# Two of four row-block transposes moved from the DMA crossbar to TensorE, and the tail loads re-slotted, in a fused attention and MLP kernel

## The chip, the cores and the metric

One NeuronCore of a Trainium2 chip runs the whole program. The metric is device microseconds of one execution. TensorE (PE in the profile), VectorE (DVE), ScalarE (ACT), GpSimd (POOL) and SyncE (SP) each work through a queue of their own in program order. Here SP only issues DMAs.

## What is computed

`q`, `k` and `v` have the shape 8 x 8 x 576 x 64 (batch, heads, sequence, head dimension), in float32. The reference does attention in a causal window of 64 positions, puts the heads side by side, and then does a residual MLP on rows of 512:

```python
mask = (rel >= 0) & (rel < 64)                      # rel = query position - key position
attn = softmax(where(mask, q @ k.T / sqrt(64), -1e9))
x = concat_heads(attn @ v)                           # 8 x 576 x 512
xn = (x - mean) / sqrt(var + 1e-6) * g_ln
out = x + relu(xn @ w_ch1) @ w_ch2                   # w_ch1 512 x 2048, w_ch2 2048 x 512
```

## The kernel before

**Groups and periods.** The rows are cut into nine groups. Groups 0 to 7 are the first 512 positions of one batch each; group 8 collects the last 64 positions of all eight batches, the "tails". A tail i (0 to 3) holds batches 2i and 2i+1 and makes one block of 128 rows of group 8. A group has four row blocks of 128. The kernel runs the groups' MLPs one after another; I call the time of one group's MLP a period. While period g runs, TensorE also does the attention of the next group b = g+1, in small pieces between the MLP's pieces.

**The MLP of a period** (`mlp_units`, from g = 2) is 30 units: 16 units of the first layer (`l1`, line 437, four 128x512 matmuls each, emptied with ReLU by ACT at line 441 into `hrT`), then 14 units of the second layer (`product`, line 513, eight 128x256 matmuls each, seven products in two halves, combined from PSUM by DVE at line 528 into `osb`). The products take sums `sw` that DVE makes (`presum`, line 427). The product tile `wX` stays in one of the two PSUM buffers of the pool `ps_t` from unit 16 to unit 29.

**Slots.** The order of everything else is written by hand: `at(i, f, ...)` puts a step behind unit i. The same order holds on all engines, because each engine runs its own instructions in the order of the program. For a row block j of the next group the steps are `s_mm` (scores, line 292), `s_exp` (ACT), `s_mask` (DVE, line 319), `b_step` (probabilities times v, line 335, then normalisation and statistics on DVE, lines 338 to 345), `r_step` (1/sqrt of the variance on ACT, lines 354 and 355), `z_step` (the normalised rows z in fp16, DVE, line 365), and a transpose of z into `zT`, which the next period's first layer reads. In `steps` the b_steps of the four blocks stand at slots 4, 8, 12 and 17, and the z_steps at 6, 10, 14 and 20.

**Two ways to transpose z.** `x_step` (line 390) has SP issue one DMA transpose of 128x512 through the crossbar. `zt_step` (line 373) has TensorE do four 128x128 transposes (line 379) into a PSUM tile `ztp` of the pool `ps_t`, and ACT copy it into `zT` (line 382). Before the change, the groups 3 to 7 and the tails use `x_step` for all four blocks; groups 0 to 2 use `zt_step`.

**The queue of SP in a period** g (2 to 5) is: loads of q and k of batch g+2 (`load_qk`, lines 83 and 90, slots 1 and 2), loads of v (`load_v`, line 152, slot 5), x_step of block 0 (slot 7), of block 1 (11), of block 2 (15), the crossbar transposes of q and k of batch g+2 (`x_main(n, 0)`, lines 245 and 251, one DMA for q and two for k, slot 18), x_step of block 3 (20), and `x_main(n, 1)` (21). A step that waits holds all that stand behind it. The casts to fp16 that `x_main` waits for are on ACT (`cast_q`, line 129, slots 16, 16, 17, 19), as are those of v (`cast_v`, slots 21 to 24), on which two copies on POOL's queue (`make_vB`, lines 180 and 181, slot 25) wait. The stores (line 398) are on POOL's queue too, two per period.

**Tails.** The dictionary `TAILS` holds the steps of the tails in periods 6 and 7: loads (`load_tail`, part 0 for q and k: lines 101 and 103, part 1 for v: line 108), casts (`cast_tail`, three per tail, for tails 0 and 3 on POOL, for tails 1 and 2 on ACT), crossbar transposes (`x_tail`, lines 261 and 262), scores and the rest. The tails' tiles share buffers with the batches' tiles: two for q, two for k, one for v.

Of the kernel before, what the change touches and what calls it, by code (L numbers as in the profile page):

```python
# [18 lines left out]
def kernel(  # L19
# [649 lines left out]
    def tail_casts(i, act, *us):  # L669
        return tuple((u, cast_tail, i, part, act) for part, u in enumerate(us))  # L670

    TAILS = {
        6: ((0, load_tail, 0, 0), (0, load_tail, 0, 1), (6, load_tail, 1, 0), *tail_casts(0, False, 8, 9, 10),
            (10, x_tail, 0), (10, load_tail, 1, 1), *tail_casts(1, True, 16, 17, 18), (18, x_tail, 1),
            (15, s_mm, 8, 0), (16, s_mask, 8, 0), (26, b_step, 8, 0),
            (15, load_tail, 2, 0), (21, load_tail, 2, 1), (23, load_tail, 3, 0),
            *tail_casts(2, True, 24, 25, 26), (25, x_tail, 2),
            (27, s_mm, 8, 1), (28, s_mask, 8, 1)),
        7: ((0, x_step, 8, 0), (1, load_tail, 3, 1), (2, b_step, 8, 1), (2, s_mm, 8, 2), (4, s_mask, 8, 2),
            (5, x_step, 8, 1), (7, b_step, 8, 2), (10, x_step, 8, 2), *tail_casts(3, False, 5, 6, 8), (8, x_tail, 3),  # L680
            (12, s_mm, 8, 3), (14, s_mask, 8, 3), (17, b_step, 8, 3), (20, x_step, 8, 3)),
    }
    for g in range(NGRP):
        units = mlp_units(g, (8, 16)[g] if g < 2 else 0, g == 0)
# [2 lines left out]
        def at(i, f, *a):  # L687
            slots[min(i, len(slots) - 1)].append((f, a))
# [6 lines left out]
        def score(u, sg, sj):  # L695
            late = u < 15
            at(u, s_mm, sg, sj, False, None, late)
            if late:
                at(u + 1, s_exp, sg, sj)
            at(u + 1 + late, s_mask, sg, sj)  # L700

        def steps(bg, bj, ub, us, sg, sj):
            if us is not None:
                score(us, bg, bj)
            late = ub < 15
            at(ub, b_step, bg, bj)
            if sj < 4:
                score(ub, sg, sj)
            at(ub + 2, r_step, bg, bj)
            at(ub + 2 + (not late), z_step, bg, bj)  # L710
            at(ub + 3, x_step, bg, bj)

        b = g + 1
        if g == 0:
# [72 lines left out]
        if g > 1 and b < B:  # L787
            for j in range(4):
                steps(b, j, (4, 8, 12, 17)[j], 0 if j == 0 else None, b, j + 1)
# [84 lines left out]
```

## Time and profile before

| what | value |
|---|---|
| seven runs | median 324.28 us (320.97 to 326.98) |
| the profiled execution, its own time | 323.74 us |
| its span in the trace | 322.0 us |
| mean granted TensorE clock | 0.983 |
| busy: PE, ACT, DVE, POOL | 294.3, 187.0, 192.7, 83.9 us |
| DMA queue of SP and ACT, share of 16 engines' span | 74.3% |

The profile comes from one execution. The table counts an engine as busy while an instruction of its own runs; matmuls are pipelined and overlap in the records. A period can be read from the timeline of PE: it begins with its first matmul of line 437. Those begin at 94.41 us for period 2, 124.67 (3), 158.15 (4), 190.66 (5), 220.72 (6), 258.67 (7) and 290.56 (8). The last matmul ends at 316.8 us.

### The profile page before, as it was taken

To read this page: it belongs to the slowest core of one execution; us is meant where nothing else is said; L and a number is where in the kernel's file an instruction comes from. 1 tells how busy PE (TensorE), PEld (TensorE's weight loads), DVE (VectorE), ACT (ScalarE), POOL (GpSimd) and SP (SyncE) were. 2 spreads that over 40 slices of the span, in tenths; PEclk is the share of its full clock that TensorE was granted. 3 is DMA by queue.
4 is the path that set the end of the run, shared out by engine and by line. 5 is a ranking of instruction groups with operands and counts; after the bars stand their busy time and mean duration, and the time that the engine had idled before them with its cause. 6 is when DMAs were issued, how large, how long until landed. Compare 5 with 4: busy or idle time off the path is not lost.

```text
span 322.0 us, 7196 instructions
## 1 busy us (share of the span) xinstructions
PE 294.3 (91%) x2903; PEld 185.2 (58%) x2903; DVE 192.7 (60%) x348; ACT 187.0 (58%) x362; POOL 83.9 (26%) x142
## 2 busy tenths in 40 slices
PE   6689998999999999999599999997987969999993
PEld 2446544856744586468244874585436834684582
DVE  0664329377867893787147945882695755671361
ACT  2799751866938873895168838871874257405600
POOL 3676756932750004001200030003040015001000
PEclk9999999999999999999779999999997999999999
DMA  7999899999989949998999589999999997103005
GB/s 178 261 385 334 298 280 294 295 263 215 177 142 284 175 87 203 256 217 122 239 265 171 67 178 253 231 134 195 218 159 181 188 257 143 33 16 130 2 2 130
DMA packets 140545, 61.67 MB, mean 192 GB/s; under 512 B 117616, under 2 KB 133488, under 8 KB 140512
## 3 DMA queue, kind: packets, MB, share of 16 engines
q1 hardware_dynamic: 136336, 49.30, 74.3%
q0 software_dynamic: 3216, 11.39, 13.2%
q10 hardware_dynamic: 960, 0.53, 0.6%
q8 instruction: 23, 0.38, 0.5%
q14 instruction: 10, 0.08, 0.1%
HBM read 38.80 MB, written 9.44 MB: 150 GB/s over the span
## 4 chain that ended last, share of the span: by engine, by line
PE 58%; DMA 12%; DVE 12%; SPq 7%; ACT 5%; issue 2%; POOL 1%; POOLq 0%; DVEq 0%; ACTq 0%
PE hps L437 28%; PE wX L513 7%; PE hph L474 5%; PE ch L450 4%; DMA qkT<-qk 3%; PE wZ L513 3%; PE sc L292 3%; PE xps L335 3%; PE ch L488 3%; DVE osb L528 3%; DMA tkT<-tk 2%; DMA zT<-z 2%; DMA w1s<-in_moe_w_ch_dram 2%; SPq L152 2%; DVE stats L343 2%
## 5 line engine op out<-in xcount | busy, mean ns | idle before, releaser
L437 PE MATMUL hps<-zT,w1g 128*128 128x512 f16 x480 | 113.8, 386 | 4.9 <-DMA zT<-z 3.6
L441 ACT ACTIVATE hrT<-hps 128x512 f16<-128x512 f32 x120 | 71.5, 597 | 56.9 <-PE hps L437 56.2
L437 PEld LDWEIGHTS <-w1g 128*128 128x128 f16 x480 | 45.3, 99 | 59.5 <-issue 12.5
L513 PEld LDWEIGHTS <-sw 128*128 128x128 f16 x448 | 43.8, 98 | 5.6 <-issue 0.5
L319 DVE TENSOR_TENSOR pt<-pt,mask 128x1024 f16<-128x1024 f16 x32 | 23.1, 723 | 33.2 <-ACT pt L306 20.4
L513 PEld LDWEIGHTS <-hrT 128*128 128x128 f16 x336 | 32.8, 100 | 5.8
L180 POOL DMA_DIRECT2D vB<-vA x6 | 3.2, 536 | 102.3 <-ACT vA L129 101.7
L398 POOL DMA_DIRECT2D out_dram<-osb x20 | 13.3, 665 | 54.2 <-DVE osb L528 42.9
L427 DVE TENSOR_TENSOR sw<-hrT 128x1024 f16<-128x1024 f16 x28 | 18.8, 671 | 12.1 <-ACT hrT L441 12.1
L306 ACT ACTIVATE pt<-sc 128x512 f16<-128x512 f32 x40 | 23.8, 595 | 3.5 <-PE sc L292 1.8
L343 DVE BATCH_NORM_STATS2 stats<-xn 128x6 f32<-128x512 f32 x36 | 25.0, 695 | 1.2
L365 DVE TENSOR_SCALAR z<-xn,mv,rs 128x512 f16<-128x512 f32 x32 | 19.9, 623 | 9.6 <-ACT rs L355 9.2
L341 DVE TENSOR_TENSOR xn<-xps,rcp 128x512 f32<-128x512 f32 x36 | 24.9, 691 | 1.2
L474 PE MATMUL hph<-zT,w1g 128*128 128x256 f16 x192 | 23.9, 273 | 1.2 <-POOL w1g L207 0.8
L312 ACT ACTIVATE pt<-sc 128x512 f16<-128x512 f32 x32 | 17.5, 596 | 8.5 <-PE sc L292 8.1
L354 ACT ACTIVATE rs<-mv,epst 128x1 f32<-128x1 f32 x36 | 10.8, 301 | 18.9 <-DVE mv L345 18.9
L474 PEld LDWEIGHTS <-w1g 128*128 128x128 f16 x192 | 17.9, 98 | 4.6 <-POOL w1g L207 1.0
L131 POOL CAST qk<-qk 128x1024 f16<-128x1024 f32 x16 | 16.6, 1039 | 12.7 <-DMA qk<-in_q_dram 6.8
L450 PE MATMUL ch<-w2s,hrT 128*128 128x512 f16 x80 | 19.8, 380 | 0.0
L335 PEld LDWEIGHTS <-pt 128*64 128x64 f16 x576 | 12.2, 110 | 12.9 <-issue 4.9
L528 DVE TENSOR_TENSOR osb<-wX,xn 128x512 f32<-128x512 f32 x21 | 14.4, 688 | 7.9 <-PE wX L513 7.9
L338 DVE RECIPROCAL rcp<-xps 128x8 f32<-128x8 f32 x36 | 7.3, 204 | 17.4 <-PE xps L335 17.3
(83 smaller groups left out, 409.2 us busy)
## 6 DMA issues: line engine op xcount, KB each, us to landing
qk<-in_q_dram SPq DMA_DIRECT2D x16, 512.0 KB, 7.1
v<-in_v_dram SPq DMA_DIRECT2D x32, 256.0 KB, 6.1
w2s<-in_moe_w_ch_dram SPq DMA_DIRECT2D x12, 512.0 KB, 6.8
out_dram<-osb POOLq DMA_DIRECT2D x12, 512.0 KB, 5.1
qk<-in_k_dram SPq DMA_DIRECT2D x20, 256.0 KB, 6.1
qk<-in_k_dram SPq DMA_DIRECT2D x6, 512.0 KB, 6.3
w1s<-in_moe_w_ch_dram SPq DMA_DIRECT2D x4, 512.0 KB, 7.3
out_dram<-osb POOLq DMA_DIRECT2D x8, 256.0 KB, 6.0
```

The lines of the kernel that those rows point to most:

```text
L306: nc.scalar.activation(out=pt[:, par].rearrange("k h w (p j) -> k (h w) p j", j=4), in_=sc[:, :].rearrange("k h w (j p) -> k (h w) p j", j=4),
L319: nc.vector.tensor_tensor(out=ptv, in0=ptv, in1=mb, op=ALU.mult)
L335: nc.tensor.matmul(out=xps[64 * r:64 * r + 64, h, :D + 1], lhsT=pt[:, par, hp, r, :], rhs=rhs, start=True, stop=True)
L341: nc.vector.tensor_tensor(out=xn, in0=xps[:, :, 0:D], in1=rcp_b, op=ALU.mult)
L343: nc.vector.bn_stats(out=stats, in_=xn.rearrange("p h d -> p (h d)"))
L365: nc.vector.tensor_scalar(out=z, in0=x, scalar1=mv[:, 0:1], scalar2=rss[(g, kb)][:, 0:1], op0=ALU.subtract, op1=ALU.mult)
L437: nc.tensor.matmul(out=hps, lhsT=w1g[:, kc, 128 * hc:128 * (hc + 1)], rhs=zT[g][:, kc, :], start=(kc == KCS[0]), stop=(kc == KCS[-1]),)
L441: nc.scalar.activation(out=hrT[:, hc, :], in_=hps, func=AF.Relu, bias=0.0, scale=1.0)
L450: nc.tensor.matmul(out=ch[kb], lhsT=hrT[:, hc, 128 * kb:128 * (kb + 1)], rhs=w2s[:, hc, :], start=(hc == 0), stop=(hc == NHC - 1),)
L474: nc.tensor.matmul(out=hps[:, e], lhsT=w1g[:, kc, 128 * hc:128 * (hc + 1)], rhs=zT[g][:, kc, 256 * half:256 * half + 256], start=(kc == KC ...
L513: nc.tensor.matmul(out=xyz[bank][:, t], lhsT=lhsT, rhs=rhs, start=bool(first and t == 0 and hc == 0), stop=(t == 1 and hc == 7), skip_grou ...
L528: nc.vector.tensor_tensor(out=o, in0=xyz[bank][:, ts], in1=x if base == "x" else o, op=ALU.add)
```

## The change

Three things change.

1. In `steps`, that is for groups 3 to 7, blocks 0 and 1 keep `x_step` at their slots 7 and 11. Blocks 2 and 3 get `zt_step` at slots 16 and 23, in place of `x_step` at 15 and 20.
2. All four blocks of the tails' group get `zt_step`, at slots 0, 6, 11 and 22 of period 7, in place of `x_step` at 0, 5, 10 and 20.
3. In the tails' lists some slots move: the casts of tail 1 one slot later (17, 18, 19) and those of tail 2 too (25, 26, 27), `x_tail(2)` from 25 to 26, the scores of tail 0 from 15 to 18 and its mask from 16 to 19, the scores of tail 2 in period 7 from 2 to 3 and its mask from 4 to 5. The q and k loads of tail 2 move from 15 to 18 and those of tail 3 from 23 to 20, the v load of tail 2 from 21 to 20, and the v load of tail 3 from slot 1 of period 7 to slot 28 of period 6.

```diff
     TAILS = {
         6: ((0, load_tail, 0, 0), (0, load_tail, 0, 1), (6, load_tail, 1, 0), *tail_casts(0, False, 8, 9, 10),
-            (10, x_tail, 0), (10, load_tail, 1, 1), *tail_casts(1, True, 16, 17, 18), (18, x_tail, 1),
-            (15, s_mm, 8, 0), (16, s_mask, 8, 0), (26, b_step, 8, 0),
-            (15, load_tail, 2, 0), (21, load_tail, 2, 1), (23, load_tail, 3, 0),
-            *tail_casts(2, True, 24, 25, 26), (25, x_tail, 2),
+            (10, x_tail, 0), (10, load_tail, 1, 1), *tail_casts(1, True, 17, 18, 19), (18, x_tail, 1),
+            (18, s_mm, 8, 0), (19, s_mask, 8, 0), (26, b_step, 8, 0),
+            (18, load_tail, 2, 0), (20, load_tail, 2, 1), (20, load_tail, 3, 0),
+            *tail_casts(2, True, 25, 26, 27), (26, x_tail, 2), (28, load_tail, 3, 1),
             (27, s_mm, 8, 1), (28, s_mask, 8, 1)),
-        7: ((0, x_step, 8, 0), (1, load_tail, 3, 1), (2, b_step, 8, 1), (2, s_mm, 8, 2), (4, s_mask, 8, 2),
-            (5, x_step, 8, 1), (7, b_step, 8, 2), (10, x_step, 8, 2), *tail_casts(3, False, 5, 6, 8), (8, x_tail, 3),
-            (12, s_mm, 8, 3), (14, s_mask, 8, 3), (17, b_step, 8, 3), (20, x_step, 8, 3)),
+        7: ((0, zt_step, 8, 0), (2, b_step, 8, 1), (3, s_mm, 8, 2), (5, s_mask, 8, 2),
+            (6, zt_step, 8, 1), (7, b_step, 8, 2), (11, zt_step, 8, 2), *tail_casts(3, False, 5, 6, 8), (8, x_tail, 3),
+            (12, s_mm, 8, 3), (14, s_mask, 8, 3), (17, b_step, 8, 3), (22, zt_step, 8, 3)),
     }
...
             at(ub + 2, r_step, bg, bj)
             at(ub + 2 + (not late), z_step, bg, bj)
-            at(ub + 3, x_step, bg, bj)
+            if bj < 2:
+                at(ub + 3, x_step, bg, bj)
+            else:
+                at((16, 23)[bj - 2], zt_step, bg, bj)
```

Counted over the program, SP loses 14 DMA transposes (10 for the groups, 4 for the tails), TensorE gains 56 transposes of 128x128 and as many weight loads, and ACT gains 14 copies of 128x512.

## The prediction

> **What bounds the kernel now.** I read the page first, then PE's timeline from period 2 on, then who waits for whom, then SP's queue. On the page PE is busy 91% of the span and no other engine over 60%. So the question is what PE waits for; in the list of waits, periods 2 to 7 put down to DMAs or to ACT behind them:
>
> ```profile
> engine line waited for: us in total, times, longest us
> ...
> PE sc L292 <- DMA tkT<-tk: 5.5, 3, 3.5
> ...
> PE hps L437 <- DMA zT<-z: 3.6, 1, 3.6
> ...
> PE sc L292 <- DMA qkT<-qk: 2.0, 2, 1.9
> ...
> PE hps L437 <- ACT hrT L441: 1.2, 1, 1.2
> ```
>
> All but the last end with a crossbar transpose, issued by SP. The stretches around the longest wait show its second price. Columns: PE, PEld, DVE, ACT and POOL busy, granted clock, DMA share, GB/s.
>
> ```profile
> 154.00:158.00 4.00, 0.56 (x6) 0.25 (x3) 0.69 (x1) 0.00 (x0) 2.25 (x5) 0.93 1.10 193
> 158.00:160.00 2.00, 1.85 (x8) 0.49 (x10) 0.00 (x0) 0.00 (x0) 0.00 (x0) 0.50 1.10 393
> 160.00:162.00 2.00, 2.00 (x21) 0.97 (x21) 0.00 (x0) 1.13 (x2) 0.00 (x0) 0.50 0.99 284
> 162.00:164.00 2.00, 2.00 (x6) 0.71 (x5) 0.47 (x1) 1.09 (x2) 0.00 (x0) 0.50 1.07 304
> ```
>
> After 3.6 us without matmuls the granted clock is 0.50 for about 6 us. SP's own timeline, for the period before that wait, says why the transpose was late:
>
> ```profile
> 135.89 6.35 SPq L152 DMA_DIRECT2D v<-in_v_dram  x4
> 142.35 4.42 SPq L390 DMA_TRANSPOSE zT<-z  x3
> 146.86 1.26 SPq L245 DMA_TRANSPOSE qkT<-qk  x1
> 148.21 2.54 SPq L251 DMA_TRANSPOSE qkT<-qk  x2
> 150.84 2.57 SPq L390 DMA_TRANSPOSE zT<-z  x1
> 153.51 1.33 SPq L245 DMA_TRANSPOSE qkT<-qk  x1
> 154.93 4.10 SPq L251 DMA_TRANSPOSE qkT<-qk  x2
> 159.08 1.22 SPq L83 DMA_DIRECT2D qk<-in_q_dram  x1
> ```
>
> SP is issuing without a pause. Block 3's transpose goes out at 150.84 and lands 7.06 us later (chain of waits), and the next loads start only at 159.08, a cycle of 31.2 us (from 127.84) against a bare TensorE period of 29.73 (period 3: 124.67 to 154.40, when its last product is issued). Other cycles of SP: 35.7, 34.4, 31.6. SP falls behind, until PE waits.
>
> What the waits cost, from PE's timeline. Period 2: 0.37. Period 3: 3.59. Period 4 lasts 32.51 without a wait, so the half clock costs 2.78 over the bare 29.73. Period 5: scores 0.74 long instead of 0.41, so 0.33. Period 6: scores 2.45 instead of 0.41, so 2.04; 3.49 for tail 0's transpose; its half clock 1.27 (scores 0.61 for 0.41, a product 2.98 for 1.91). Period 7: 1.16 + 1.70 + 0.31 = 3.17. Sum 17.04 us. That is the most there is to win.
>
> **The change, part by part.**
>
> *PE gains 14 groups of four transposes.* The same operation in period 1 shows its price inside a full stream: the next matmul starts 0.22 later.
>
> ```profile
> 87.22 0.39 PE L379 MATMUL ztp<-ident,z 128*128 128x128 f16 x4
> 87.44 1.89 PE L450 MATMUL ch<-w2s,hrT 128*128 128x512 f16 x8
> ```
>
> So 14 x 0.23 = 3.2 us, all on the path; upper end 14 x 0.40 = 5.6, the whole record each time. I take the lower, since all 14 stand in full streams.
>
> *PE waits for z of block 2.* Slot 16 is behind the first half of the first product. In period 3 that half is issued at 141.68 + 0.87 = 142.55, but z is there at 143.10:
>
> ```profile
> 142.56 0.54 DVE L365 TENSOR_SCALAR z<-xn,mv,rs 128x512 f16<-128x512 f32 x1
> ```
>
> DVE is busy without a pause before it, so z comes no sooner. The hold is 0.55, in periods 2, 4 and 5 by the same sum 0.63, 0.63 and 0.62 (z done at 112.92, 179.45 and 209.50; the product begins at 111.42, 177.95 and 208.01), in 6, where no score would stand before it (z at 241.19, the layer's end at 239.87), 0.45: together 2.9 us for five periods. The second product half and block 3's values times v are queued behind. Ends: 2.3 (0.45 each) and 4.5 (0.9, if DVE slips by its next 0.7 us instruction in two periods). Block 3's z is done at 148.44 and slot 23 is reached at 149.15 + 0.87 = 150.0 at the earliest: 1.6 us of slack, no wait.
>
> *ACT gains 14 copies* of 0.587 (the row of L382), 8.2 us. ACT is busy 20.6 of 30.3 us in period 2, and in the products of period 3 it idles after 150.5. The copy of block 2 stands ahead of ACT's casts of q and k: they start about 1.6 us later than 142.53 (PE at 143.5, then the copy). Who waits for them is `x_main` on SP, which is issued at 146.86 and 153.51 now; the casts would end at about 145.1 (first q) and 147.1 (second q). Price 0 for PE while SP is earlier by more than this; gone that cover, 1.6 us per period. In period 7 three copies stand between ACT's ReLUs; ACT is busy there 14.8 of 34.7 us, so 0, at most 1.8.
>
> *SP loses 14 issues* of 1.19 to 2.68 us and, what is more, the holds in front of them: it no longer waits for z of blocks 2 and 3. `x_main` can follow the casts: q of the second half at about 149 instead of 153.5, and it lands within 5.2 to 5.8 us (its rows in the chain), so by 155, about when the next period starts. The loads behind start some 4 us sooner, at or before the next period. Blocks 0 and 1, still on SP, went out 9 us or more before the period's end even now. So I expect the waits of periods 3 and 5, and the 2.04 of period 6, to go, with the half clock of period 4.
>
> *DMA engines.* A transpose of 131 KB alone (284 to 286 us: share 0.32 of 2 us) takes 0.64 us of all 16, so two less are 1.3 us per period of 30 to 33 busy. Ends: 0.64 and 1.3 each (under load the 16 engines moved 81 GB/s at a share of 0.80 from 150 to 154, half the speed).
>
> *Tails.* SP reached tail 0's load at 225.09, 4.4 us into period 6, and its transposes at 237.76 to 241.4, behind a transpose of z; PE stood until 243.43. With SP 4 us or more early and two issues fewer, the transposes follow POOL's casts (paced by ReLUs 8 and 9), and scores three slots later give 2.6 us more: 3.49 and the clock's 1.27 go. The three moved slots only move PE's 0.41 us. Tail 2's q and k, though at slot 18 instead of 15, no longer stand behind two transposes of z; `x_tail(2)` went out at 258.20, and now follows its casts at slots 25 and 26. By my reckoning it lands 1 to 2 us ahead of slot 3 of period 7, so the 1.70 goes. Tail 3's loads, two slots and eight slots earlier, wait for buffers that ACT's casts of tail 1 and 2 free; behind them on SP stands only `x_tail`. Left over: ACT waited 4.24 us for tail 2's v (DVE's and PE's 1.16 behind it); v lands earlier but its cast is one slot later, so I keep 0.5 of 1.16. And tail 0's mask at slot 19 holds DVE until the scores' exponentials are done, with the additions that free `wX` behind it: 0.4, as the 0.37 that PE waited for DVE in period 2. Ends of this remainder: 0 and 3.2 (today's sum of period 7).
>
> **Sum.** 17.04 - 3.2 - 2.9 - 0.9 = 10.0 us gained. The profiled execution took 323.74, so 313.7. It stands 0.54 under the median of the runs, so against the median 314.2. Periods 3 to 5 should last 29.73 + 0.46 + 0.6 = 30.8, period 6 about 32, period 7 about 30.
>
> Two pages of the Trainium skill speak against this. "VectorE: DVE Perf Modes", The three transpose paths, puts a 128x128 transpose on TensorE at 390 ns. The row says 219 ns each and 0.22 for four in a row; by the page 56 would cost 21.8 us, and the sum would be a loss of 8.6. "Advanced Engine Details and Errata", X-Bar Transpose, says that transposing DMAs are as fast as ordinary ones. Here the lone one ran at about 205 GB/s; by the page (350 GB/s or more) it would take 0.37 us, the relief of the engines would be under 0.8 us per period, and the gain would rest on SP's order alone.
>
> **Rivals.**
>
> *One wait stays* (chance 0.20). A 7.06 us landing is a full DMA system, not a late issue alone; the share from 154 to 158 is 1.10. If one period still starts with the long wait and its half clock (3.59 + 2.78), or the tails keep as much, the time is 314.2 + 6.4 = 320.6. Against it: the share drops to 0.43 from 150 to 152, so the engines have pauses.
>
> *It doesn't reach the bound* (0.11). If landing is set by the DMA engines alone, periods 3 to 6 keep 3.59 + 2.78 + 0.33 + 2.04 = 8.7, and only the tails win: 314.2 + 8.7 = 322.9, no change. For it: the loads are issued at 1.6 us per 256 KB, well over the shortest 0.37.
>
> *Slower* (0.07): the casts behind block 2's copy become the late link. The place is the first scores of periods 3 to 6. Each wait of w there costs four times w; over 2.5 us each the gain is gone. At 4 us each: 314.2 + 16 = 330.2, more with half clocks. Against it: the casts slip by 1.6, SP frees 4.
>
> **How the numbers follow.** The likeliest case has 0.62 and a range of its own of 312.6 to 317.5. Its lower end takes 3.1 and 2.3 for the transposes and holds and no remainder (324.28 - 17.04 + 5.4); its upper end takes any one of 5.6, 4.5 and 3.2 with half of another (314.2 + 2.4 + 0.9). With the rival at 320.6 the cases hold 0.82. Below, the range goes to where block 2's hold would be nothing too, 324.28 - 17.04 + 3.1 = 310.3, and so it is 310.3 to 321. A measurement here tells about 1% from no change: faster means under 321.0. The first case and 0.19 of the second's 0.20 lie there, 0.81; within 1% are 0.01 and the 0.11 of no change, 0.12; slower 0.07.
>
> **What would show it.** Right: no wait of PE for zT; 104 records of `ztp` on PE and 26 copies on ACT; PE waiting for z (L365) about 0.6 us five times; no slice of the clock under 9 after 94 us; SP's loads starting at or before each period; no tkT waits; 3 to 5 at 30.8 us. Wrong: qkT taking zT's place at the start of a period; a half clock anywhere; periods over 31.5; ACT's casts late; PE held over 1 us at slot 16, or at tail 2's scores.

## The result, and the profile after

| | before | after |
|---|---|---|
| median (runs) | 323.74 us (64) | 319.17 us (27) |
| lowest to highest | 319.15 to 328.61 | 316.52 to 322.94 |
| profiled execution | 323.74 us, span 322.0 | 317.87 us, span 315.8 |

The ratio of after to before is 0.9897, with a 95% interval of 0.9875 to 0.992. The ratio counts only the runs within 1.5% of the fastest of their kernel; the quotient of the medians of all runs is 0.986. So the change is faster by about 1%, where 314.2 us (3%) were forecast, in a range of 310.3 to 321.0. The time lies in the range, but the gain is a third (by the ratio) to a half (by the medians) of the forecast one. Where it went is read best from the starts of the periods on PE's timeline (first matmul of line 437), in the two profiled executions:

| length, us | period 2 | 3 | 4 | 5 | 6 | 7 | from period 8 to the end of the span |
|---|---|---|---|---|---|---|---|
| before | 30.26 | 33.48 | 32.51 | 30.06 | 37.95 | 31.89 | 31.4 |
| after | 30.77 | 30.78 | 30.77 | 30.78 | 32.14 | 34.93 | 31.6 |
| forecast | not given | 30.8 | 30.8 | 30.8 | about 32 | about 30 | not given |

Periods 3 to 6 came as forecast, to 0.2 us. Period 7, the one of the tails, was forecast to become 2 us shorter and became 3 us longer. The list of waits of the kernel after, put beside that of before in the prediction, shows both:

```profile
engine line waited for: us in total, times, longest us
...
PE ztp L379 <- DVE z L365: 3.1, 7, 0.8
...
PEld L292 <- DMA tkT<-tk: 2.6, 1, 2.6
...
PE sc L292 <- DMA tkT<-tk: 2.1, 1, 2.1
...
PE hps L437 <- ACT hrT L441: 1.3, 1, 1.3
```

No wait of PE for zT or qkT is left. The new wait for z is the forecast hold in front of block 2's transposes (five of its seven times are the holds at slot 16). What stays is one wait for a transpose of a tail's k, and one for ACT. SP's timeline for period 3 shows the queue ahead of its work. Before, the loads in its last line started at 159.08, 4.5 us behind 154.56, where PE began to wait for zT and could have begun the next period; here they start at 154.11, 1.5 us ahead of the next period (155.58):

```profile
139.55 3.73 SPq L390 DMA_TRANSPOSE zT<-z  x2
145.28 1.23 SPq L245 DMA_TRANSPOSE qkT<-qk  x1
146.60 2.55 SPq L251 DMA_TRANSPOSE qkT<-qk  x2
149.24 1.26 SPq L245 DMA_TRANSPOSE qkT<-qk  x1
150.60 3.46 SPq L251 DMA_TRANSPOSE qkT<-qk  x2
154.11 1.36 SPq L83 DMA_DIRECT2D qk<-in_q_dram  x1
```

PE's timeline at slot 16 of the same period shows the price on TensorE. The transposes wait 0.43 us for z by the record, and the next half of the product follows 0.23 after they begin:

```profile
141.82 1.04 PE L513 MATMUL wX<-w2s,hrT 128*128 128x256 f16 x8
143.29 0.40 PE L379 MATMUL ztp<-ident,z 128*128 128x128 f16 x4 [0.43 <-DVE z L365]
143.52 1.04 PE L513 MATMUL wX<-w2s,hrT 128*128 128x256 f16 x8
```

What the hold costs is more than 0.43. The idle time in brackets is counted from the end of the last matmul's record, and in an unbroken stream the next instruction begins before that end: in period 7 of the same timeline a half product that begins at 278.09, its record 1.04 long too, is followed at 278.96, 0.87 later. Here the two halves begin 1.70 apart (141.82 and 143.52). Without 0.87 for the first half and 0.23 for the transposes, 0.60 is left for the hold.

In period 7, PE's timeline has two holes, 1.34 and 2.06 us, close together (the fence runs on to the instruction behind them):

```profile
252.72 1.02 PE L437 MATMUL hps<-zT,w1g 128*128 128x512 f16 x4 [1.34 <-ACT hrT L441]
254.05 1.04 PE L437 MATMUL hps<-zT,w1g 128*128 128x512 f16 x4
257.15 0.41 PE L292 MATMUL sc<-tqT,tkT 64*128 64x64 f16 x16 [2.06 <-DMA tkT<-tk]
257.49 4.45 PE L437 MATMUL hps<-zT,w1g 128*128 128x512 f16 x12
261.78 0.39 PE L379 MATMUL ztp<-ident,z 128*128 128x128 f16 x4
```

and behind them the granted clock is 0.50 again (stretches; the column behind POOL is the clock):

```profile
257.00:259.00 2.00, 1.85 (x21) 0.90 (x22) 0.00 (x0) 0.69 (x2) 0.00 (x0) 0.76 1.17 334
259.00:261.00 2.00, 2.00 (x6) 0.76 (x5) 1.04 (x2) 1.77 (x5) 0.00 (x0) 0.50 0.55 89
```

The twelve first-layer matmuls that begin at 257.49 take 4.29 us to the next instruction, where twelve at full clock take 2.6: 1.7 us more. So period 7 is the 28.7 that it took before without its waits (31.89 - 3.17), four times 0.23 for transposes, the holes 1.34 + 2.06, a hold of 0.17 and the half clock 1.7: 34.9. SP's timeline says what stood ahead of tail 2's transposes (lines 261 and 262):

```profile
245.68 1.83 SPq L101 DMA_DIRECT2D tq<-in_q_dram  x2
247.55 1.64 SPq L103 DMA_DIRECT2D tk<-in_k_dram  x2
249.31 3.27 SPq L261 DMA_TRANSPOSE tqT<-tq  x1
252.68 1.25 SPq L262 DMA_TRANSPOSE tkT<-tk  x1
```

The two loads are tail 3's q and k, which the change puts at slot 20. ACT had cast tail 2's q by 245.74 and its k by 248.43, but the transposes go out at 249.31 and 252.68, and the second lands 4.4 us later.

The loads stood there before the change too; SP's timeline of the kernel before has the same order:

```profile
254.69 1.74 SPq L101 DMA_DIRECT2D tq<-in_q_dram  x2
256.47 1.63 SPq L103 DMA_DIRECT2D tk<-in_k_dram  x2
258.20 2.40 SPq L261 DMA_TRANSPOSE tqT<-tq  x1
```

So relative to the start of period 7 tail 2's first transpose goes out no sooner than before: 0.04 behind it (249.27), where it was 0.47 ahead of it (258.67).

### The profile page after: what moved, and what is told of

It reads as the page before. It is cut to its first block, busy times and chain, and to the rows that moved or that the text cites. A ratio compares the mean times of both kernels' runs of the same rounds, so it can differ in the third digit from the quotient of the medians.

```text
span 315.8 us, 7287 instructions
## 1 busy us (share of the span) xinstructions
PE 296.1 (94%) x2959; PEld 186.9 (59%) x2959; DVE 192.8 (61%) x348; ACT 194.5 (62%) x376; POOL 83.3 (26%) x142
## 4 chain that ended last, share of the span: by engine, by line
PE 73%; DVE 10%; DMA 6%; SPq 4%; ACT 3%; issue 1%; POOL 1%; ACTq 0%
PE hps L437 28%; PE wX L513 13%; PE wZ L513 7%; PE hph L474 5%; PE wY L513 4%; PE ch L450 4%; PE xps L335 3%; PE sc L292 3%; PE ch L488 3%; DMA w1s<-in_moe_w_ch_dram 3%; SPq L152 2%; DVE sw L427 2%; DVE stats L343 2%; DVE xn L341 2%; PE ztp L379 2%; DMA tv<-in_v_dram 2%
## 5 line engine op out<-in xcount | busy, mean ns | idle before, releaser
L319 DVE TENSOR_TENSOR pt<-pt,mask 128x1024 f16<-128x1024 f16 x32 | 23.8, 745 | 25.0 <-ACT pt L312 12.6
L513 PEld LDWEIGHTS <-hrT 128*128 128x128 f16 x336 | 32.0, 98 | 5.4
L382 ACT COPY zT<-ztp 128x512 f16<-128x512 f16 x26 | 15.3, 587 | 18.6 <-PE ztp L379 18.5
L365 DVE TENSOR_SCALAR z<-xn,mv,rs 128x512 f16<-128x512 f32 x32 | 18.8, 588 | 8.3 <-ACT rs L355 8.1
```

Of the source, the lines that this page charges most:

```text
L319: nc.vector.tensor_tensor(out=ptv, in0=ptv, in1=mb, op=ALU.mult)
L365: nc.vector.tensor_scalar(out=z, in0=x, scalar1=mv[:, 0:1], scalar2=rss[(g, kb)][:, 0:1], op0=ALU.subtract, op1=ALU.mult)
L513: nc.tensor.matmul(out=xyz[bank][:, t], lhsT=lhsT, rhs=rhs, start=bool(first and t == 0 and hc == 0), stop=(t == 1 and hc == 7), skip_grou ...
```

## Experiments

My theory after the result had two parts. The groups' part gains by SP's order (not by lighter DMA engines), and the tails' lists give it back, because tail 3's loads stand on SP ahead of tail 2's transposes. The rivals: the DMA engines' load is what counts, in the groups and in the tails; or the tails' lists are needed for period 6.

### The two halves alone

`groups_only` has the edit of `steps` and the old `TAILS`; `tails_only` the new `TAILS` and the old line in `steps`.

> Only the transposes of blocks 2 and 3 of groups 3 to 7 go to TensorE; the tails' lists are as before. My theory: the gain of periods 3 to 6 comes from these alone, and the tails' lists of the change cost period 7 what it lost. Then periods 2 to 5 last 30.8 us each, period 6 about 34.5 (scores of tail 0 stand at slot 15, about 3 us before its transpose can land), period 7 about 32 as before; span 315 to 317, so as fast as the change within 0.5%. Rival: without the new tail lists period 6 keeps its 37.9, and the span is 319 or more.

Measured: median 316.22 us, ratio 0.9839 (0.9745 to 0.9932), span 313.6. Periods 2 to 5 take 123.05 together, period 6 35.64 (about 34.5 was expected), period 7 29.16 (about 32 was expected). So the groups' part alone was no slower than the whole change, as expected; whether it is faster the intervals, which overlap, don't tell. Period 7 is 2.7 under before. PE's timeline of this kernel shows what the old lists cost, the wait in period 6 at slot 15, and how little is left for tail 2:

```profile
237.14 0.61 PE L292 MATMUL sc<-tqT,tkT 64*128 64x64 f16 x16 [2.59 <-DMA tkT<-tk]
...
256.39 0.41 PE L292 MATMUL sc<-tqT,tkT 64*128 64x64 f16 x16 [0.20 <-DMA tkT<-tk]
```

Tail 2's scores start at 256.39 here and at 257.15 in the change. The absolute time is nearly the same; the change only arrives there 1.1 us sooner, and waits. What the change wins over this kernel in period 6 (32.14 for 35.64), PE stands still for in period 7.

> Only the tails' part of the change; groups 3 to 7 keep all four crossbar transposes. My theory: SP stays behind, so periods 2 to 5 take 126 us together as before (30.3 + 33.5 + 32.5 + 30.1), period 6 about 35, and period 7 34 or more, because tail 2 is at least as late as in the change; span 321 to 324, no faster than before. Rival: the tails' lists bring a gain of their own, and the span is under 319.

Measured: median 321.81, ratio 1.0017 (0.9971 to 1.0064), span 319.2, so no faster than before, as expected. But periods 2 to 5 took 123.3 us here and not 126, with the old groups. Its waits at the starts of periods were 0.42 (zT), 1.17 and 1.79 (qkT), and none was followed by a half clock. So the profiled execution of before, which the forecast was built on, may not be typical. Period 6 took 33.90, less than the 35 expected, and period 7 37.04. The reason expected for the last, a late tail 2, did not show: PE waited there 2.95 us for ACT (hrT), and not for tail 2's transposes.

### SP's order or the DMA engines' load

Both kernels are the change with the crossbar transposes of blocks 2 and 3 put back, into a tile `zx` that nobody reads. `xq_hold` puts them at the old slots, `xq_end` behind `x_main` (another line of it keeps the tile z in `zkeep` until then). The lines below are of both kernels; each has its own.

```diff
+    def x_dummy(g, kb, z):
+        t = p_grp.tile([128, NKC, 128], FP16, tag="zx", name=f"zx_{g}_{kb}")
+        nc.sync.dma_start_transpose(out=t, in_=z)
...
             else:
+                at(ub + 3, lambda: x_dummy(bg, bj, zsd[(bg, bj)]))          # xq_hold
                 at((16, 23)[bj - 2], zt_step, bg, bj)
+                at(24, lambda: x_dummy(bg, bj, zkeep[(bg, bj)]))            # xq_end
```

> The change, and beside it SP still issues the crossbar transposes of blocks 2 and 3 at their old slots 15 and 20, into a tile that nobody reads (work is added, the output is the same). So SP has its old holds and the DMA engines their old load, but the next period's first layer doesn't wait for them. If SP's order was the cause (my theory), x_main and the loads are as late as before, and PE waits for qkT at the start of some periods (0.3 to 2 us each, periods 5 and 6); periods 3 to 5 together 93 to 95 us instead of 92.3. If only the late landing of zT itself mattered, periods stay at 30.8 us.

Measured: median 325.32 us of four runs, no interval; span 321.6. One wait for qkT at the start of period 4 came back, 1.52 us, where some in periods 5 and 6 were expected; the other periods of 2 to 5 stay near 30.8. Periods 3 to 5 take 93.99, inside what was expected. Period 7 took 38.95, with waits of 3.05 us for z and 2.40 for ACT, which this run alone does not explain.

```profile
158.34 0.29 PE L292 MATMUL sc<-qkT,qkT 64*128 64x64 f16 x8 [1.52 <-DMA qkT<-qk]
```

> The change, and beside it SP issues the two crossbar transposes behind x_main, at slot 24, into a tile that nobody reads (work is added, the output is the same). The DMA engines have their old load (0.64 us of all 16 for each), but nothing on SP is held by z. If SP's order was the cause, periods 2 to 5 stay at 30.8 us. If the load on the DMA engines was the cause, waits for qkT or v come back, and periods 3 to 5 take 1 us more each.

Measured: median 322.66, ratio 1.0019 (0.9969 to 1.0069), span 321.0. Periods 3, 4 and 5 take 30.76, 30.77 and 30.76, with no wait for a DMA. SP's timelines show what differs: the q transpose of the second half, in period 3, goes out at 149.33 here and at 149.24 in the change, but at 152.74 in `xq_hold` and at 153.51 before. So in the groups the two transposes' load on the DMA engines cost PE nothing in this execution, and the holds on SP cost 1.7 us in one period of four in the other. That speaks for SP's order; with one execution of each and waits that move from one execution to the next (below), it is a weak test. The kernel lost its time in the tails: periods 6 and 7 took 32.98 and 39.27. Its two added transposes stand on SP at 252.70 to 256.33, ahead of tail 2's at 256.43, which go out 7 us later than in the change (249.31):

```profile
261.79 0.61 PE L292 MATMUL sc<-tqT,tkT 64*128 64x64 f16 x16 [3.95 <-DMA tkT<-tk]
```

### The tails

`load3_late` moves tail 3's loads of q and k behind tail 2's transposes.

```diff
-            (18, load_tail, 2, 0), (20, load_tail, 2, 1), (20, load_tail, 3, 0),
-            *tail_casts(2, True, 25, 26, 27), (26, x_tail, 2), (28, load_tail, 3, 1),
+            (18, load_tail, 2, 0), (20, load_tail, 2, 1),
+            *tail_casts(2, True, 25, 26, 27), (26, x_tail, 2), (27, load_tail, 3, 0), (28, load_tail, 3, 1),
```

> The change, with the q and k loads of tail 3 moved from slot 20 to 27, so that on SP they stand behind the transposes of tail 2 and not ahead of them. My theory: in period 7 PE waits 2.06 us for tkT of tail 2 because SP issues those loads first; with them behind, the transposes follow ACT's cast (248.4 in the change) at once and land at about 253, before slot 3 is reached (255.1). The 2.06 us go, and the half clock behind them (1.7), because 1.33 us alone are too short for it: period 7 falls from 34.9 to about 31.2, span 312. Rival: the DMA engines are full there (share over 1.1 from 244 to 258) and the landing is set by them, not by the order on SP; then the wait falls by less than 1 us and the half clock stays.

Measured: median 314.12, ratio 0.9725 (0.968 to 0.977), span 313.4 with period 2 starting 0.45 later than in the change. Period 7 takes 32.10 instead of 34.93. SP's timeline shows the new order, PE's what is left:

```profile
246.96 1.68 SPq L261 DMA_TRANSPOSE tqT<-tq  x1
249.57 2.65 SPq L262 DMA_TRANSPOSE tkT<-tk  x1
252.27 1.35 SPq L101 DMA_DIRECT2D tq<-in_q_dram  x2
253.67 1.85 SPq L103 DMA_DIRECT2D tk<-in_k_dram  x2
```

```profile
253.32 1.02 PE L437 MATMUL hps<-zT,w1g 128*128 128x512 f16 x4 [1.45 <-ACT hrT L441]
...
255.92 0.41 PE L292 MATMUL sc<-tqT,tkT 64*128 64x64 f16 x16 [0.23 <-DMA tkT<-tk]
```

k's transpose goes out 3.1 us sooner, the wait falls from 2.06 to 0.23, and the clock stays at 1.00 from 252 to 264. Its landing took 6.3 us from the issue and not 4.4, so part of what SP's order won was lost again behind the issue. The interval of the ratio lies clear of the change's (0.9875 to 0.992), so the order of these two loads is shown to cost the change most of what it missed. That the median meets the 314.2 that was forecast is luck in part: period 7 still took 2 us more than forecast, and the forecast took off waits that not every execution has (below). Period 7 came out at 32.1 and not 31.2. The wait for ACT, which that figure held at 1.33, was 1.45, 0.23 was left of the wait for tail 2, and block 2's transposes of the tails waited 0.40 for z instead of 0.17; that is 0.6 of the 0.9.

`v2_late` leaves SP's order as in the change and moves ACT's cast of tail 2's v.

```diff
-            *tail_casts(2, True, 25, 26, 27), (26, x_tail, 2), (28, load_tail, 3, 1),
+            *tail_casts(2, True, 25, 26), (26, x_tail, 2),
-        7: ((0, zt_step, 8, 0), (2, b_step, 8, 1), ...
+        7: ((0, zt_step, 8, 0), (1, cast_tail, 2, 2, True), (1, load_tail, 3, 1), (2, b_step, 8, 1), ...
```

> The change, with ACT's cast of tail 2's v moved from slot 27 of period 6 to slot 1 of period 7 (and the v load of tail 3 behind it), so that the exponentials of tail 1's scores and the first ReLUs no longer stand behind a cast that waits for a load (landed at 250.0). The wait of 1.33 us for hrT goes. But then slot 3 is reached 1.3 us sooner, and the wait for tkT of tail 2 grows by as much, to about 3.4 us, with a half clock: period 7 stays at 34 to 35, no gain. Rival: the waits add, and period 7 loses 1.3 us.

Measured: median 319.32, ratio 0.9883 (0.9844 to 0.9923), span 317.4, as fast as the change. The wait for ACT is gone, and the wait for tail 2 took its place:

```profile
258.60 0.61 PE L292 MATMUL sc<-tqT,tkT 64*128 64x64 f16 x16 [5.19 <-DMA tkT<-tk]
```

It is 5.19 and not 3.4 us, since the transpose also landed 1.5 us later than in the change: its tkT went out at 252.77, only 0.1 later, and took 5.8 us instead of 4.4. The same landing took 6.0 us in a second execution of the unchanged change (`after_again`, below), so this part need not come from the edit. Period 7 took 36.67, more than the 34 to 35 expected. That the two waits are one chain, and not a sum, holds.

`both_late` has both edits.

> Both of the moves before: tail 3's q and k loads behind tail 2's transposes, and the cast of tail 2's v behind the exponentials. By my theory both waits and the half clock go: period 7 about 29.8 to 30.5 instead of 34.9, span 311. Rival: the waits only move to tail 3's chain (its loads are later by 7 slots), and period 7 stays over 32.

Measured: median 314.17, ratio 0.9755 (0.9688 to 0.9822), span 311.8. Period 7 takes 30.53, as expected, and only tail 3's scores wait, 0.79. By the spans it is 1.6 us better than `load3_late`; the medians don't tell the two apart.

### Block 2's hold

`zt2_17` puts block 2's transposes one slot later.

```diff
-                at((16, 23)[bj - 2], zt_step, bg, bj)
+                at((17, 23)[bj - 2], zt_step, bg, bj)
```

> The change, with block 2's transposes on TensorE at slot 17 instead of 16, that is behind the second half of the first product. The hold of 0.43 us for z (five times in the change) goes, periods 2 to 5 last 30.35 instead of 30.78, and the gain is 0.43 x 5 = 2.1 us, if ACT's casts, 0.45 us later still, stay off the path. Rival: DVE or ACT hands the 0.43 on to a later wait, and the periods stay at 30.78.

Measured: median 316.59, ratio 0.9797 (0.9756 to 0.9838), span 314.0. Periods 3 to 5 take 30.16 each, 0.61 under the change and not 0.43: it is the whole hold of 0.60 that the starts of the two halves show. Its PE timeline has the transposes behind the whole product, with no wait in front of them:

```profile
141.10 1.91 PE L513 MATMUL wX<-w2s,hrT 128*128 128x256 f16 x16
142.85 0.39 PE L379 MATMUL ztp<-ident,z 128*128 128x128 f16 x4
```

Period 7 took 36.27, with waits of 1.89 for ACT and 1.70 for tail 2: the periods before are shorter, the tail's chain isn't.

### All three moves

`best` is `both_late` with slot 17.

> The change with all three moves: block 2's transposes at slot 17, tail 3's q and k loads behind tail 2's transposes, the cast of tail 2's v behind the exponentials. If the three terms add, periods 2 to 5 last 30.16 as in the run with slot 17, period 6 31.5, period 7 about 30.5 as in the run with both tail moves; span 311.8 - 5 x 0.6 = 309, a time of 311, ratio to before 0.962. If ACT's casts or SP's order give it back in the tails (period 6 is 0.6 shorter, the loads no earlier), a wait for tkT of tail 2 or 3 of 1 to 3 us comes, and the span is 311 to 312.

Measured: median 311.84, ratio 0.9658 (0.9606 to 0.9711), span 310.1, faster than both kernels. Periods 3 to 5 take 30.16 and period 6 31.53, the terms add; period 7 takes 31.85 instead of 30.53, for PE reaches tail 2's scores 2.3 us sooner and waits again:

```profile
252.71 0.41 PE L292 MATMUL sc<-tqT,tkT 64*128 64x64 f16 x16 [1.12 <-DMA tkT<-tk]
```

So 1.3 of the 3 us went back to the same chain. The wait is the one of the expectation's second branch; the span lies between its two branches, 309 and 311 to 312.

### Further executions of the two kernels

> The kernel before, unchanged, a second execution with a trace. It tells whether the long wait for zT at the start of period 4 (3.59 us, and 2.78 for the half clock) that the prediction put into the gain is in each execution. If the schedule makes it, it is there again within 1 us. If it is an event of one execution, periods 2 to 5 take about 123.3 us together as they did in the run with the tails' part alone, and not 126.3.

> The kernel before, unchanged, a third execution with a trace, for the same question: which waits of periods 2 to 7 recur, and with what size. SP's cycle of 31 to 36 us against a period of 29.7 is expected in each; where PE meets it (zT, qkT, tkT) may differ.

> The change, unchanged, a second execution with a trace. The periods of 30.78 us and the hold of 0.43 us for z are set by the schedule and should recur within 0.1 us; period 7 should again be over 33 us, with a wait for tkT of tail 2 of 1 to 4 us, as SP issues tail 3's loads ahead of it.

| one execution, lengths in us | time | periods 2 to 5 | period 6 | period 7 |
|---|---|---|---|---|
| before, as profiled first | 323.74 | 126.3 | 37.95 | 31.89 |
| before_again | 319.70 | 122.9 | 37.95 | 31.51 |
| before_third | 324.96 | 123.1 | 37.79 | 36.10 |
| after, as profiled first | 317.87 | 123.1 | 32.14 | 34.93 |
| after_again | 320.69 | 123.1 | 32.14 | 37.73 |

The wait of 3.59 us for zT with its half clock is in one of the three executions. PE's timeline of before_third has 0.73 and 1.79 for zT instead, and a wait of 4.06 for qkT early in period 6:

```profile
155.53 1.02 PE L437 MATMUL hps<-zT,w1g 128*128 128x512 f16 x4 [0.73 <-DMA zT<-z]
...
188.05 1.04 PE L437 MATMUL hps<-zT,w1g 128*128 128x512 f16 x4 [1.79 <-DMA zT<-z]
...
223.09 0.40 PE L292 MATMUL sc<-qkT,qkT 64*128 64x64 f16 x8 [4.06 <-DMA qkT<-qk]
```

With `tails_only`, three of four executions with the old groups spend 122.9 to 123.3 us in periods 2 to 5, as much as the change's 123.1. Which period waits differs; in these three the sum hardly does. Period 6 is the same in each execution of a kernel, to 0.2 us. Period 7 is not settled by the schedule alone in either kernel: its wait for tail 2 was 2.06 us in one execution of the change and 3.69 in the other, and in before_third ACT held PE 3.14 us there.

## Why the prediction was right and wrong

**The bound** was right in the main: PE's waits for crossbar transposes issued by SP, and the half clock behind them. `load3_late` and `both_late` won time by moving these alone or with ACT's wait beside them; `zt2_17` won its part by the hold for z.

**PE's 14 groups of transposes** (3.2 us, 0.23 each): right; 0.23 again in the change.

**The hold for block 2's z** (0.45 to 0.63, together 2.9): right. The records show 0.43 of idle time, but PE lost 0.60 in each of five periods, 3.0 us, and slot 17 gave back 0.61 per period.

**ACT's copies, price 0 for PE in the groups**: right. The first q went out on SP at 145.28, where 145.1 was reckoned for its cast.

**SP's order and the waits of periods 3 to 6**: right for the profiled execution, to 0.2 us a period. `xq_end` and `xq_hold` speak for the order and against the relief of the engines, which the prediction reckoned without giving it a term; one execution of each is not proof. Wrong was to take one execution's waits for the kernel's: 17.04 us, "the most there is to win", held 3.59 + 2.78 for one wait that the other two executions of before don't have at that length; they are 3.2 and 3.4 us shorter in these periods. There, and in `tails_only`, periods 2 to 5 cost 122.9 to 123.3 against 123.1, so the groups win nothing in these periods: the waits that go are worth no more than the transposes and holds that come. The gain that recurs is period 6, 37.8 to 37.95 against 32.14 in both executions of the change; `groups_only` has 35.64 there.

**The tails** failed, and this is the step that the forecast broke on: that `x_tail(2)` "now follows its casts" and lands "1 to 2 us ahead of slot 3 of period 7, so the 1.70 goes". The prediction saw that "behind them", tail 3's loads, "on SP stands only `x_tail`", and gave that no price. But that `x_tail` is tail 2's, and its landing is what PE waits for in period 7. With the 3.5 us of the loads ahead of it, it went out 3.6 us behind its cast of q (249.31 for 245.74) and landed 2.06 behind slot 3, with a half clock of 1.7; and 1.34 were left for ACT where 0.5 was kept. The other 0.4 that the prediction kept, for tail 0's mask, did not come: PE has no such wait in period 6. Period 7 was 34.9 and not about 30. `load3_late` takes 2.8 us of that back by this one move. The wait is an old one: the loads stood ahead of tail 2's transposes before the change too, and what is won in period 6 arrives at the same landing and stands there. `groups_only`, which loses 3.5 us in period 6, meets tail 2 at nearly the same time (256.39 against 257.15) and ends 2.2 us sooner than the change, by the spans of one execution each.

**The rivals**: what came is nearest to the first, a wait that stays with its half clock, "or the tails keep as much", at 320.6. It had 0.20. The slower case (ACT's casts) left no trace, and the case of no gain in the groups came true for periods 2 to 5 in three of four executions with the old groups, by another road: not since landing is set by the engines, but since the waits were smaller than in the one profile.

## What to carry to other kernels

When a step stands in a queue that works in order, look for what stands behind it and who waits for that, even if the step itself has time to spare and was there before. A wait that is taken away early in a chain comes back at the next landing that did not move; reckon the landing in absolute time, not relative to the period. And before waits of one trace are added up as a gain, look at a second execution: here the same kernel spent 126.3, 122.9 and 123.1 us in the same four periods.

## What the runs showed that I had not expected

A single wait's length doesn't tell whether the half clock follows. After 2.22 us without matmuls (before_again, period 6) the clock stayed at 1.00, after 2.59 (groups_only) the scores took 0.61 for 0.41. But in before_again waits of only 0.20 and 1.38 us, with 1.2 us of work between them, were followed by it:

```profile
156.00:158.00 2.00, 0.92 (x10) 0.43 (x10) 0.00 (x0) 0.71 (x2) 0.96 (x4) 0.86 1.09 359
158.00:160.00 2.00, 2.00 (x6) 0.76 (x5) 0.00 (x0) 0.88 (x2) 0.00 (x0) 0.50 1.09 341
160.00:162.00 2.00, 2.00 (x8) 0.79 (x7) 0.69 (x1) 1.01 (x3) 0.00 (x0) 0.78 0.66 111
```

The Trainium skill, "TensorE: Matmul & The Clock Gate", Part 1, says that the gate watches a window of 3.4 us that runs free of the program. That would let equal waits end differently, and these runs don't speak against it; none of them tests it. They do show the half clock behind single waits shorter than 3.4 us (2.59). In the change, two holes of 1.34 and 2.06 us, 2.4 us of work apart, cost 1.7 us more than themselves, while 1.45 and 0.23 in `load3_late` were followed by a full clock.
